# Packed attention products half a step later behind the apart tokens' values, the second scores two half steps later, and the turned blocks' splits ahead of the weights'

## The chip, the cores and the metric

The kernel runs on one core of a Trainium2 chip. The metric is device time in microseconds (us) of one execution; the times before are three runs, 954.72, 954.94 and 955.8 us, with a median of 954.94 us. The engines are TensorE (PE, with its weight loads as PEld), VectorE (DVE), ScalarE (ACT), GpSimd (POOL) and SyncE (SP), which issues most of the DMAs.

## What is computed

Two attention stages in a row (32 packed queries attend to 576 keys, then the 576 queries attend to the 32 packed results), then a two-dimensional Fourier transform over tokens and channels, a normalisation and a two-layer network:

```python
p_packed = sm_attn(p, k, v)                 # 8 batches x 8 heads, 32 packed queries, 576 keys, 64 channels
out = sm_attn(q, p_packed, p_packed)
x = out.transpose(0, 2, 1, 3).reshape(8, 576, 512)
mixed = np.real(np.fft.fft(np.fft.fft(x, axis=1), axis=2))
u = x + mixed
un = (u - mean(u)) / np.sqrt(var(u) + 1e-6)
return u + np.maximum(un @ w_ch1, 0.0) @ w_ch2        # 512 -> 2048 -> 512
```

The kernel keeps about full fp32 accuracy in the network by splitting each operand into a high and a low part and making three matmuls out of one.

## The kernel before

The rows of u are cut into 36 blocks of 128: four for each of the 8 batches (even and odd combinations of tokens), and one for every pair of batches with the 2 x 64 "apart" tokens that fit into no other block. Four blocks make a tile of 512 rows, so there are 9 tiles, 0 to 8. `ffn` runs the network over one tile: for j from 0 to 15, `up(j)` makes 12 matmuls of 128x512 (`ph`, line 958) and `down(j - 1)` 12 more (`acc`, line 977). After each `up` and each `down` stands a call of `step`, so that a tile has 32 half steps, 0 to 31: `step(2j)` lies between `up(j)` and `down(j - 1)`, `step(2j + 1)` between `down(j - 1)` and `up(j + 1)`.

In these half steps the attention and the Fourier transform of the next batch are woven in. `front(b)` is a generator, and each `step` asks it for its next piece; the string `ORDER` says which pieces come, with "y" for the end of a half step. In tile t, `front(t + 1)` runs this way, and two half steps are given to the end of `front(t)` instead: the apart tokens' spectra and their values. The letters of the string for batches from 2 on that matter here:

- V, S, D: load the values, scores of the packed queries, scores out to memory and back turned (`e1T`, two tensors of four DMAs each; the first is issued by SP, the second by ACT in half step 2)
- p0, p1: `packed`, the product of the turned scores with the values (`po`, line 434), normalised by DVE into `pp` (line 439) for each of the two groups of heads
- d0, d1: `packed_parts`, a transpose on PE (`pptp`, line 454), copies and splits of it (`ppT`, `pph`, `ppl`)
- g0, g1: `values_spectrum`, matmuls `pg` (lines 521 and 522), two multiplications on DVE for each (`turned`, line 529) and, one half step later, a split by ACT and POOL (`gh`, `gl`)
- U: `queries`, the second scores (`s2Tt`, `s2T`, line 338) and their transposes on DVE (line 480)
- e, m: the softmax's maximum, exponential and mean

The apart tokens' values are `px<-bd,fa` (line 693), with `xa` and `ubuf` on DVE behind them (lines 714 and 865), and for odd batches a sum for the statistics (line 867). Each `packed`, `pptp`, `pg`, `px` or score takes a PSUM bank out of a ring of three by the name `ps`; `ph` has one bank and `acc` four. The order on PE, DVE, ACT and POOL is the order of the program; SP's is a scheduler's.

At the end of a tile the next tile's blocks are split: `send` (DVE lines 882 and 885, then DMAs `far` and `back`) has turned most of them through memory in half steps 4, 5, 12 and 27, and `parts(i)` makes `uh` on ACT and `ul` on DVE (lines 107 and 110) out of `back`. The weights are split all along, twice for each j: `wr_h` on ACT, `wr_l` on POOL (also lines 107 and 110), with buffers for three pairs.

Of the kernel before, what the change touches and what calls it, by code (L numbers as in the profile page):

```python
# [14 lines left out]
ALU = mybir.AluOpType  # L15
AX = mybir.AxisListType

P = 128
S = 576
HS = S // 2  # L20
D = 64
NPK = 32
# [19 lines left out]
         "i20 d1 w1 m0 q1 e1 T3 a0 f0 i120 g0 j0 r0 w2 w3 c0 w4 w5 i40 g1 m1 P0 w6 X0 j1 a1 f1 c1 r1 P1 X1 v2 W10 P2 w7 T2",  # L42
         "K0 K1 Q0 Q1 y S V0 V1 y X y p0 p1 y d0 d1 y g0 y U y g1 y e0 y e1 y y m0 y a0 y m1 y a1 y f0 y r0 y h0 y f1 y r1 y "
         "h1 y y",
         "V0 V1 S D y X Q0 Q1 y p0 p1 y d0 d1 y g0 y U y g1 y e0 y e1 y y m0 y a0 y m1 y a1 y f0 y r0 y h0 y f1 y r1 y "
         "h1 y y")


# [35 lines left out]
def tile_kernel(ctx, tc, kpT, qT, v, w1, w2, tabS, tabH, tabL, tabR, tabF, tabB, tabT, sel, ident_d, out):  # L84
    nc = tc.nc
# [151 lines left out]
    now = {}  # L237
# [54 lines left out]
    def front(b):  # L292
        kps, vts, qts, e1s, e1T, rinv, away = {}, {}, {}, {}, {}, {}, {}
# [131 lines left out]
        def packed(g):  # L425

            if g not in vts:
                load_values(g)
            vt = vts[g]
            po = bank("po")  # L430
            for c in range(5):
                kk = chunk_rows(c)
                for h in range(4):
                    nc.tensor.matmul(  # L434
                        po[h * NPK:(h + 1) * NPK, :D], e1T[g][:kk, h, c, :],
                        vt[c][:kk, h * D:(h + 1) * D], start=(c == 0), stop=(c == 4),
                        tile_position=(0, h * NPK))
            pp2 = work.tile([P, 2, D], F32, tag="pp2", name="pp2")
            nc.vector.tensor_scalar(pp2, po[:, :D].unsqueeze(1).to_broadcast([P, 2, D]), rinv[g], None, ALU.mult)
            pp2s[g] = pp2  # L440

            def spread():
                mask, n = (bpair, 2) if b else (bmask, 4)
                bd[g] = work.tile([P, n, D], F32, tag=f"bd{n}", name="bd")
                nc.gpsimd.tensor_tensor(bd[g], pp2[:, 0:1, :].to_broadcast([P, n, D]), mask.unsqueeze(2).to_broadcast([P, n, D]),
                                        ALU.mult)

            in_place("b", g, spread)
# [477 lines left out]
    def wsplits():  # L926

        for t, _ in enumerate(tiles):
            for n, j in [(0, 0)] + [x for j in range(1, NJ) for x in ((0, j), (1, j - 1))] + [(1, NJ - 1)]:
# [4 lines left out]
                yield  # L934

    def ffn(first, turned, step, nxt, alone):
        keys = turned.keys
        n = len(keys)
        T = n * P
        uh, ul = turned.hl  # L940
        acc = [psf.tile([P, DM], F32, tag=f"acc{i}", name=f"acc{i}") for i in range(n)]
        now["acc"] = acc

        def up(j, moves=(), between=lambda: None):
            moves = list(moves)
            wh, wl = ready.pop(0)

            pool, tag = (ps, "ps") if alone and j % 2 else (psf, "ph")
            ph = pool.tile([P, 512], F32, tag=tag, name="ph")

            step = T // 2 if first == 0 and j < SPL else T
            for t in (slice(i, i + step) for i in range(0, T, step)):
                for k in range(12):
                    if step < T:
                        c, (l, r) = k % 4, ((wh, uh), (wl, uh), (wh, ul))[k // 4]
                    else:
                        c, (l, r) = k // 3, ((wh, uh), (wh, ul), (wl, uh))[k % 3]
                    nc.tensor.matmul(ph[:, t], l[:, c * P:(c + 1) * P], r[:, c, t], start=(k == 0), stop=(k == 11))  # L958
                    if moves:
                        moves.pop(0)()  # L960
            between()
            hh = ffp.tile([P, 512], F32R, tag="hh", name="hh")
            hl = ffp.tile([P, 512], F32R, tag="hl", name="hl")
            nc.scalar.activation(hh[:, :T], ph[:, :T], AF.Relu)  # L964
            nc.vector.scalar_tensor_tensor(hl[:, :T], ph[:, :T], 0.0, hh[:, :T].bitcast(F32), ALU.max, ALU.subtract)  # L965
            return hh, hl

        def down(j, hh, hl, moves=(), pair=None, to=range(n)):

            moves = list(moves)  # L970
            vh, vl = pair or ready.pop(0)
            for i in to:
                w = slice(i * P, (i + 1) * P)
                halved = nxt is None and j == NJ - 1 and i == n - 1
                for cols in (slice(0, DM // 2), slice(DM // 2, DM)) if halved else (slice(0, DM),):
                    for k, (l, r) in enumerate(((hh, vh), (hh, vl), (hl, vh))):
                        nc.tensor.matmul(acc[i][:, cols], l[:, w], r[:, cols], start=(j == 0 and k == 0),  # L977
                                         stop=(j == NJ - 1 and k == 2 and cols.stop == DM))
                        if moves:
                            moves.pop(0)()  # L980

        def less(*ks):
            for k in ks:
                nxt.less(k)

        def sends(i):
            for _ in range(SENDS.count(i) if nxt is not None else 0):
                nxt.send_next()  # L990

        prev = None
        for j in range(NJ):
            last = nxt is not None and j == NJ - 1
            if last:
                late = [i for i in range(4) if i not in nxt.sent]
                assert len(late) in (0, 1, 2, 4), late
                early = late[:2] if len(late) == 4 else []
                late = [i for i in late if i not in early]
                cur = up(j, [m for i in early for m in nxt.moves(i)], lambda: less(*late))  # L1000
                ahead = [i for i in range(4) if i not in late]
                for i in ahead[:2]:
                    nxt.parts(i)
            else:
                cur = up(j, [lambda: None] * 7 + [turn_others] if first + j == 0 else ())
            next(splits, None)
            if nxt is not None and j == NJ - 2 and not nxt.sent:
                less(0, 1)
            step(2 * j)
            sends(2 * j)  # L1010
            if nxt is None and j == NJ - 1:
                pairs = [ready.pop(0), None]
                down(j - 1, *prev, pair=pairs[0], to=(0, 1))
                pairs[1] = ready.pop(0)
                for k, i in ((1, 0), (1, 1), (0, 2), (1, 2), (0, 3), (1, 3)):
                    down(j - 1 + k, *(prev, cur)[k], pair=pairs[k], to=(i,))
                break
            if prev is not None:
                down(j - 1, *prev, [lambda: None] * 8 + nxt.moves(late[0]) if last and late else ())
                if last:  # L1020
                    for i in ahead[2:]:
                        nxt.parts(i)
                next(splits, None)
                if last:
                    for i in late[:1]:
                        nxt.parts(i)
            step(2 * j + 1)
            sends(2 * j + 1)
            prev = cur
        if nxt is not None:  # L1030
            down(NJ - 1, *prev, nxt.moves(late[1]) if len(late) > 1 else ())
            if len(late) > 1:
                nxt.parts(late[1])
            next(splits, None)
        for i in (2, 3, 0, 1) if nxt is not None else range(4):
            u = u_of[keys[i]]
            for cols in (slice(0, DM // 2), slice(DM // 2, DM)) if nxt is None and i == 3 else (slice(0, DM),):
                nc.vector.scalar_tensor_tensor(u[:, cols], acc[i][:, cols], stat_of[keys[i]][:, 2:3], u[:, cols],  # L1038
                                               ALU.mult, ALU.add)
                (nc.sync if cols.start == 0 else nc.scalar).dma_start(out[(first + i) * P:(first + i + 1) * P, cols], u[:, cols])  # L1040
            free.append(place_of[keys[i]])
# [50 lines left out]
    rest = gen0  # L1092
    for t, (first, tk) in enumerate(tiles):

        gen = gens.pop(t + 1, None) or (front(t + 1) if t + 1 < B else iter(()))
        ended = []

        def step(i):

            next_step()  # L1100
            if i == 2 and t + 1 < B and t:
                now.pop("back")()
            if i in ((1, 2) if t else (0, 2)):
                next(rest, None)
            elif not ended and next(gen, None) == "rest":
                ended.append(gen)
            if t == 0:
                load_weights(i)
            assert i < 2 * NJ - 1 or t + 1 >= B or ended

        nxt = Turned(tiles[t + 1][1]) if t + 1 < len(tiles) else None

        with tc.manual_schedule(engines=MANUAL):
            ffn(first, cur, step, nxt, t + 1 >= B)
        cur, rest = nxt, gen
# [114 lines left out]
```

## Time and profile before

| what | value |
|---|---|
| median of three runs | 954.94 us (954.72 to 955.8) |
| the profiled execution | 953.94 us, of which its span is 952.1 us |
| PE busy | 938.0 us, 99% of the span, 5593 matmuls |
| DVE, ACT, POOL busy | 60%, 47%, 48% |
| DMA, mean | 85 GB/s |
| granted TensorE clock | 0.998 |
| chain that ended last | PE 93%, DMA 2%, DVE 2%, ACT, POOL and issue 1% each |

Matmuls are pipelined, so that a matmul row's duration (some 0.39 us for 128x512) is longer than the distance to the next row's start. The time that a matmul takes from the kernel is read from starts. In the rows of the timeline the first number is the start in us, the second the duration, then engine, line, operation, output and inputs, shapes, a count, and in brackets the idle time just before with what ended it. Tile 0 starts at about 41.7 us, tile 1 at 149.5, tile 2 at 253.8, and the others at 358.2, 461.5, 564.7, 668.0, 771.3 and 860.2 us.

### The profile page before, as it was taken

What the parts mean: (1) busy time and instruction counts of PE and PEld (TensorE: products, weight loads), DVE (VectorE), ACT (ScalarE), POOL (GpSimd) and SP (SyncE); (2) the same over time, 40 slices, a digit from 0 to 9 for tenths busy, and PEclk for the clock granted to TensorE, in tenths of its full rate; (3) what the DMA queues carried; (4) which work ended last, traced back from release to release, by engine and by line L of the source; (5) the groups of instructions that cost most, each with busy time, mean ns of one, the idle gap of its engine ahead of it and who ended that gap; (6) DMA issues with size and microseconds to landing.
All of it is one profiled execution on the core that took longest, in us unless ns stands there. A gap on an engine that the chain in (4) does not pass through costs nothing.

```text
span 952.1 us, 15116 instructions
## 1 busy us (share of the span) xinstructions
PE 938.0 (99%) x5593; PEld 759.1 (80%) x5593; DVE 574.4 (60%) x1171; ACT 444.1 (47%) x909; POOL 453.9 (48%) x392
## 2 busy tenths in 40 slices
PE   7899999999999999999999999999999999999998
PEld 5678887788778887788778877888778878888886
DVE  6789866594758656784678476864678453123112
ACT  4798564444534454444543454454344443233231
POOL 4456444553445444553554354544455355445442
PEclk9999999999999999999999999999999999999999
DMA  9793225200450016200540045100610011001001
GB/s 356 241 349 111 70 88 197 76 1 1 145 175 1 0 53 217 72 1 34 170 138 1 1 144 174 46 1 25 211 41 12 22 46 45 23 23 45 1 0 45
DMA packets 49305, 81.00 MB, mean 85 GB/s; under 512 B 7121, under 2 KB 29137, under 8 KB 49233
## 3 DMA queue, kind: packets, MB, share of 16 engines
q1 hardware_dynamic: 42896, 69.82, 21.8%
q10 hardware_dynamic: 5328, 8.98, 3.0%
q0 software_dynamic: 1008, 1.25, 0.5%
q8 instruction: 44, 0.72, 0.3%
q14 instruction: 29, 0.23, 0.1%
HBM read 59.71 MB, written 20.32 MB: 84 GB/s over the span
## 4 chain that ended last, share of the span: by engine, by line
PE 93%; DVE 2%; DMA 2%; ACT 1%; POOL 1%; issue 1%; ACTq 0%; SPq 0%; DVEq 0%; POOLq 0%
PE acc L977 41%; PE ph L958 40%; PE px L693 2%; PE po L434 1%; DMA w1f<-w 1%; PE py L289 1%; PE py L288 1%; PE py L290 1%; PE py L743 1%; DMA e1T<-fare 1%; PE s2T L338 1%; PE s L338 0%; ACT e L365 0%; PE pz L635 0%; PE pz L658 0%
## 5 line engine op out<-in xcount | busy, mean ns | idle before, releaser
L110 POOL TENSOR_TENSOR wr_l<-w2f,wr_h 128x512 fp32r<-128x512 f32 x144 | 188.4, 1308 | 289.3 <-ACT wr_h L107 267.3
L110 POOL TENSOR_TENSOR wr_l<-w1f,wr_h 128x512 fp32r<-128x512 f32 x144 | 195.3, 1356 | 186.4 <-ACT wr_h L107 160.2
L965 DVE SCALAR_TENSOR_TENSOR hl<-ph,hh 128x512 fp32r<-128x512 f32 x144 | 99.5, 691 | 297.8 <-ACT hh L964 295.4
L977 PE MATMUL acc<-wr_h,hh 128*128 128x512 f32 x577 | 228.5, 396 | 0.0
L958 PE MATMUL ph<-uh,wr_h 128*128 128x512 f32 (+1 forms) x580 | 225.9, 391 | 1.0 <-ACT uh L107 1.0
L977 PE MATMUL acc<-wr_l,hh 128*128 128x512 f32 x577 | 225.3, 390 | 0.0
L977 PE MATMUL acc<-wr_h,hl 128*128 128x512 f32 x577 | 225.1, 390 | 0.0
L958 PE MATMUL ph<-ul,wr_h 128*128 128x512 f32 (+1 forms) x580 | 224.3, 388 | 0.4 <-DVE ul L110 0.4
L958 PE MATMUL ph<-uh,wr_l 128*128 128x512 f32 (+1 forms) x580 | 224.1, 388 | 0.0
L964 ACT ACTIVATE hh<-ph 128x512 fp32r<-128x512 f32 x144 | 86.1, 598 | 243.1 <-PE ph L958 242.8
L107 ACT CAST wr_h<-w1f 128x512 fp32r<-128x512 f32 x144 | 89.3, 620 | 179.8 <-POOL wr_l L110 80.3
L958 PEld LDWEIGHTS ph<-uh,wr_h 128*128 128x128 f32 x580 | 108.5, 188 | 29.1 <-DVE s L480 5.9
L977 PEld LDWEIGHTS acc<-wr_h,hh 128*128 128x128 f32 x577 | 108.3, 188 | 25.3 <-issue 1.6
L977 PEld LDWEIGHTS acc<-wr_h,hl 128*128 128x128 f32 x577 | 108.3, 188 | 23.2
L958 PEld LDWEIGHTS ph<-uh,wr_l 128*128 128x128 f32 x580 | 108.5, 188 | 22.7
L958 PEld LDWEIGHTS ph<-ul,wr_h 128*128 128x128 f32 x580 | 108.6, 188 | 21.7 <-DVE ul L110 0.8
L977 PEld LDWEIGHTS acc<-wr_l,hh 128*128 128x128 f32 x577 | 108.4, 188 | 21.0
L107 ACT CAST wr_h<-w2f 128x512 fp32r<-128x512 f32 x144 | 88.2, 612 | 36.7 <-PE acc L977 23.3
L266 POOL TENSOR_TENSOR stat<-stat,mhalf 128x1 f32<-128x1 f32 x36 | 28.1, 792 | 0.0
L1038 DVE SCALAR_TENSOR_TENSOR ubuf<-acc,stat,ubuf 128x512 f32<-128x512 f32 (+1 forms) x37 | 25.0, 731 | 2.9 <-PE acc L977 2.9
L262 ACT ACTIVATE junk<-ubuf,stat 128x512 f32<-128x512 f32 x36 | 25.8, 717 | 0.1
L110 DVE TENSOR_TENSOR ul<-back,uh 128x512 fp32r<-128x512 f32 x28 | 25.1, 935 | 0.5 <-ACT uh L107 0.2
(222 smaller groups left out, 1081.8 us busy)
## 6 DMA issues: line engine op xcount, KB each, us to landing
kp<-kpT SPq DMA_DIRECT2D x16, 608.0 KB, 5.0
out<-ubuf SPq DMA_DIRECT2D x35, 256.0 KB, 4.0
far<-unt SPq DMA_DIRECT2D x28, 256.0 KB, 2.0
back<-far SPq DMA_DIRECT2D x112, 64.0 KB, 2.0
qt<-qT ACTq DMA_DIRECT2D x12, 576.0 KB, 4.7
vt<-v SPq DMA_DIRECT2D x12, 512.0 KB, 3.9
w1f<-w SPq DMA_DIRECT2D x9, 512.0 KB, 5.6
w2f<-w SPq DMA_DIRECT2D x9, 512.0 KB, 5.8
```

Of the source, the lines that this page charges most:

```text
L107: copied = nc.scalar.copy(hi, src)
L110: (lo_eng or nc.vector).tensor_tensor(lo, src, hi.bitcast(F32), ALU.subtract)
L262: nc.scalar.activation(junk, u, AF.Square, bias=st[:, 1:2], scale=-sign, accum_out=st[:, 2:3])
L266: nc.gpsimd.tensor_tensor(st[:, 2:3], st[:, 2:3], mhalf, ALU.pow)
L288: nc.tensor.matmul(o, lh, rh, start=first, stop=False)
L289: nc.tensor.matmul(o, lh, rl, start=False, stop=False)
L693: nc.tensor.matmul(banks[r][rows, k * 256 + g * P:k * 256 + (g + 1) * P], x[g][at, w], bd[g][at].rearrange("p a d -> p (a d)"), start=True ...
L958: nc.tensor.matmul(ph[:, t], l[:, c * P:(c + 1) * P], r[:, c, t], start=(k == 0), stop=(k == 11))
L964: nc.scalar.activation(hh[:, :T], ph[:, :T], AF.Relu)
L965: nc.vector.scalar_tensor_tensor(hl[:, :T], ph[:, :T], 0.0, hh[:, :T].bitcast(F32), ALU.max, ALU.subtract)
L977: nc.tensor.matmul(acc[i][:, cols], l[:, w], r[:, cols], start=(j == 0 and k == 0), stop=(j == NJ - 1 and k == 2 and cols.stop == DM))
L1038: nc.vector.scalar_tensor_tensor(u[:, cols], acc[i][:, cols], stat_of[keys[i]][:, 2:3], u[:, cols], ALU.mult, ALU.add)
```

## The change

Three edits. First, the string for batches from 2 on gets another "y" ahead of p0, so that p moves from half step 4 to 5, d from 5 to 6, g0 from 6 to 7, and U from 7 to 9; g1 stays in 8, e0 and e1 move by one half step to 10 and 11, and m0 and all behind it stay. Second, for tiles from 1 on the piece of the apart tokens' values moves from half step 2 to 5, where it comes ahead of p, and `packed` writes both groups of heads into two column ranges of one bank, with both normalisations behind the second group. Third, at the end of a tile all blocks that were turned through memory are split at once, ahead of the weights' next split, where two of them came behind it.

```diff
-         "V0 V1 S D y X Q0 Q1 y p0 p1 y d0 d1 y g0 y U y g1 y e0 y e1 y y m0 y a0 y m1 y a1 y f0 y r0 y h0 y f1 y r1 y "
+         "V0 V1 S D y X Q0 Q1 y y p0 p1 y d0 d1 y g0 y g1 y U y e0 y e1 y m0 y a0 y m1 y a1 y f0 y r0 y h0 y f1 y r1 y "
...
-            po = bank("po")
+            if g == 0 or b < 2:
+                po = now["po"] = bank("po")
+            else:
+                po = now["po"]
+            po = po[:, g * D:(g + 1) * D]
...
+            if b < 2:
+                normalized(g, po)
+            elif g == 1:
+                for k in range(2):
+                    normalized(k, now["po"][:, k * D:(k + 1) * D])
+
+        def normalized(g, po):
+
             pp2 = work.tile([P, 2, D], F32, tag="pp2", name="pp2")
-            nc.vector.tensor_scalar(pp2, po[:, :D].unsqueeze(1).to_broadcast([P, 2, D]), rinv[g], None, ALU.mult)
+            nc.vector.tensor_scalar(pp2, po.unsqueeze(1).to_broadcast([P, 2, D]), rinv[g], None, ALU.mult)
...
-                for i in ahead[:2]:
+                for i in ahead:
                     nxt.parts(i)
...
-                if last:
-                    for i in ahead[2:]:
-                        nxt.parts(i)
...
-            if i in ((1, 2) if t else (0, 2)):
+            if i in ((1, 5) if t else (0, 2)):
                 next(rest, None)
-            elif not ended and next(gen, None) == "rest":
+            if i not in ((1, 2) if t else (0, 2)) and not ended and next(gen, None) == "rest":
                 ended.append(gen)
```

On PE, in tile 5, the apart tokens' values stood alone between `up(1)` and `down(0)` before:

```order
L958 MATMUL ph<-uh,wr_h 128x512
L958 MATMUL ph<-ul,wr_h 128x512
L958 MATMUL ph<-uh,wr_l 128x512
L693 MATMUL px<-bd,fa 64x128 x4
L977 MATMUL acc_6271<-wr_h,hh 128x512
L977 MATMUL acc_6271<-wr_l,hh 128x512
```

and the packed products between `up(2)` and `down(1)`; of the change both stand, one behind the other, between `down(1)` and `up(3)` (lines 705, 438, 989 and 970 are the old 693, 434, 977 and 958):

```order
L989 MATMUL acc_6270<-wr_h,hh 128x512
L989 MATMUL acc_6270<-wr_l,hh 128x512
L989 MATMUL acc_6270<-wr_h,hl 128x512
L705 MATMUL px<-bd,fa 64x128 x4
L438 MATMUL po<-vt,e1T 32x64 x16
L438 MATMUL po<-vt_6294,e1T 32x64 x4
L438 MATMUL po<-vt,e1T 32x64 x16
L438 MATMUL po<-vt_6298,e1T 32x64 x4
L970 MATMUL ph<-uh,wr_h 128x512
```

Two places where the network's matmuls are interrupted have become one. On DVE in the same tile the rows from the apart tokens' values to the next `hl` are now these (`xa`, `ubuf` and `stat` belong to the apart tokens, `pp` normalises the packed products, `unp` and `unt` are a send):

```order
L726 TENSOR_TENSOR xa<-px,spec_6360 64x2x128 x2
L877 TENSOR_TENSOR ubuf<-xa,spec_6362 64x256 x2
L879 TENSOR_REDUCE stat<-ubuf 128x1
L257 TENSOR_SCALAR stat<-stat 128x1
L451 TENSOR_SCALAR pp_6518<-po,ri 128x128
L451 TENSOR_SCALAR pp_6522<-po,ri 128x128
L894 TENSOR_SCALAR unp<-ubuf,stat 128x512
L897 STREAM_TRANSPOSE unt<-unp 128x512
L977 SCALAR_TENSOR_TENSOR hl<-ph,hh 128x512
L468 COPY ppT<-pptp 128x128
```

Before, the two normalisations had the `hl` of an `up` ahead of them and the apart tokens' rows stood one `hl` earlier. On ACT at the end of tile 7 the order was

```order
L964 ACTIVATE hh<-ph 128x512
L107 CAST uh<-back 128x4x128 x2
L107 CAST wr_h<-w1f 128x512
L107 CAST uh<-back 128x4x128 x2
L107 CAST wr_h<-w1f 128x512
L107 CAST wr_h<-w2f 128x512
```

and is now

```order
L976 ACTIVATE hh<-ph 128x512
L107 CAST uh<-back 128x4x128 x4
L107 CAST wr_h<-w1f 128x512 x2
L107 CAST wr_h<-w2f 128x512
L976 ACTIVATE hh<-ph 128x512
```

so that the four high parts follow each other and the first weights' split comes two casts later.

More of the change, by code (lines that the diff above doesn't have):

```diff
@@ L434, in packed @@
                     nc.tensor.matmul(
-                        po[h * NPK:(h + 1) * NPK, :D], e1T[g][:kk, h, c, :],
+                        po[h * NPK:(h + 1) * NPK], e1T[g][:kk, h, c, :],
                         vt[c][:kk, h * D:(h + 1) * D], start=(c == 0), stop=(c == 4),
                         tile_position=(0, h * NPK))
+            if b < 2:
[4 more added lines that the diff above has]
+        def normalized(g, po):
             pp2 = work.tile([P, 2, D], F32, tag="pp2", name="pp2")
-            nc.vector.tensor_scalar(pp2, po[:, :D].unsqueeze(1).to_broadcast([P, 2, D]), rinv[g], None, ALU.mult)
+            nc.vector.tensor_scalar(pp2, po.unsqueeze(1).to_broadcast([P, 2, D]), rinv[g], None, ALU.mult)
             pp2s[g] = pp2
```

## The prediction

> **What bounds the kernel now.** First the page's busy times, then the chain of waits, then PE's timeline at the places that the change touches.
>
> ```profile
> span 952.1 us, 15116 instructions
> PE 938.0 (99%) x5593; PEld 759.1 (80%) x5593; DVE 574.4 (60%) x1171; ACT 444.1 (47%) x909; POOL 453.9 (48%) x392
> ```
>
> PE is busy 99% of the span and no other engine over 60%, so the end is set by the sequence of PE's matmuls, and only two things can shorten it: a wait of PE that goes, or a matmul that is spaced more closely to the next. The chain of waits gives the spacing where nothing interrupts:
>
> ```profile
> 456.21 5.44 PE acc L977 x24
> ```
>
> 24 matmuls of 128x512 take 5.44 us, 0.2267 us each. Whatever exceeds this at an interruption is its cost. No matmul is added or removed by the change, so I look for excess.
>
> **Edit 1, the packed products half a step later: a wait goes.** PE's timeline at the packed products of tiles 1, 2 and 4:
>
> ```profile
> 163.49 0.77 PE L434 MATMUL po<-vt,e1T 128*32 128x64 f32 x40
> ...
> 165.28 0.50 PE L977 MATMUL acc<-wr_h,hh 128*128 128x512 f32 x1
> ...
> 267.77 0.77 PE L434 MATMUL po<-vt,e1T 128*32 128x64 f32 x40
> 269.00 0.77 PE L434 MATMUL po<-vt,e1T 128*32 128x64 f32 x40 [0.46 <-DMA e1T<-fare]
> 269.70 0.50 PE L977 MATMUL acc<-wr_h,hh 128*128 128x512 f32 x1
> ...
> 475.42 1.34 PE L434 MATMUL po<-vt,e1T 128*32 128x64 f32 x80
> 476.69 0.50 PE L977 MATMUL acc<-wr_h,hh 128*128 128x512 f32 x1
> ```
>
> In tile 4 the 80 matmuls take 476.69 - 475.42 = 1.27 us; in tile 2 they take 1.93, because the second group's turned scores land late, and in tile 1 they take 1.79. The excess is 0.66 and 0.52, together 1.18 us. (The bracket shows only 0.46, since a row's modelled end hides part of the gap.) Tiles 3 to 6 have no such wait. With the products behind `down(1)` PE comes some 2.72 us (12 matmuls) and the apart tokens' 0.58 (below) later, less the interruption of half step 2 that has gone. That is over 2 us more for a DMA that is 0.7 us late at most. Its issue does not move: it stands in half step 2 on ACT, behind work of half steps 0 and 1. **Term: -1.18 us.** From both sides: 0 if something moved the DMA as well, -1.18 if the wait goes whole; I take -1.18, since 2 us of cover is three times the wait.
>
> **Edit 2, the apart tokens' values in front: one interruption less.** The same view in tile 4, at the values of half step 2:
>
> ```profile
> 468.85 0.39 PE L958 MATMUL ph<-uh,wr_l 128*128 128x512 f32 x1
> 469.17 0.65 PE L693 MATMUL px<-bd,fa 64*64 64x128 f32 x8
> 469.75 0.50 PE L977 MATMUL acc<-wr_h,hh 128*128 128x512 f32 x1
> ...
> 472.60 0.39 PE L958 MATMUL ph<-uh,wr_h 128*128 128x512 f32 x1
> ```
>
> From the last `ph` to the next `up` pass 472.60 - 468.85 = 3.75 us. They hold 13 full matmuls (13 x 0.2267 = 2.95) and the values' own 469.75 - 469.17 = 0.58. The rest, 0.22 us, is paid for going from full matmuls to tiles of the array and back: 469.17 - 468.85 = 0.32 instead of 0.23 going in, and 0.13 spread over the first full matmuls afterwards. The packed products pay the same when alone. If the two stand together, one pair of these is saved, provided that the seam between a 64*64 and a 128*32 tiling costs nothing. The trace has no such seam, but a like one, 64*32 scores followed by 128*32 strips, beside each of them alone:
>
> ```profile
> 464.43 1.06 PE L338 MATMUL s<-kp 64*32 64x512 f32 x16
> 465.43 0.64 PE L658 MATMUL pz<-ysum,tbf 128*32 128x258 f32 x8
> 466.00 0.51 PE L650 MATMUL pz<-yr,tbr 101*128 101x258 f32 x2
> ...
> 486.00 1.06 PE L338 MATMUL s2T<-qt,ppT 64*32 64x512 f32 x16
> 487.00 0.50 PE L958 MATMUL ph<-uh,wr_h 128*128 128x512 f32 x1
> ...
> 774.09 0.64 PE L658 MATMUL pz<-ysum,tbf 128*32 128x258 f32 x8
> 774.67 0.51 PE L650 MATMUL pz<-yr,tbr 101*128 101x258 f32 x2
> ```
>
> Scores take 1.00 us to the next start whether strips follow (465.43 - 464.43) or a full matmul (487.00 - 486.00); the strips take 0.57 behind scores and 0.58 behind a full matmul (tile 7, where no scores precede). So the seam is free, and a group that joins another adds only its body. Both pieces exist in tiles 1 to 6 (tile 7 has no next batch). **Term: 6 x 0.22 = -1.3 us.** From both sides: 0 if the seam costs as much as what it replaces, -1.3 if it is free; I take the like seam's answer.
>
> The Trainium skill, page "TensorEngine Tiling (Array Packing)", section "Key Properties", says that changing the tiling mode drains TensorE, which speaks against a free seam: three changes of mode would stand where four stood, so that half of the 0.22 were saved, 0.7 us in all. In the trace a tiled group's time to the next start is the same before either kind of successor, so that a drain, if there is one, is already in the group's own body.
>
> **What these moves put on other engines.** Everything that moves is issued one or two half steps later with the same successors, so I check who is late next, in tile 5, where an odd batch has the most on DVE:
>
> ```profile
> 574.29 0.77 DVE L714 TENSOR_TENSOR xa<-px,spec 64x256 f32<-64x256 f32 x2
> 575.09 0.95 DVE L865 TENSOR_TENSOR ubuf<-xa,spec 64x256 f32<-64x256 f32 x2
> 576.08 0.69 DVE L867 TENSOR_REDUCE stat<-ubuf 128x1 f32<-128x512 f32 x1
> ...
> 580.08 0.60 DVE L439 TENSOR_SCALAR pp<-po,ri 128x128 f32<-128x128 f32 x2
> 580.60 0.95 DVE L882 TENSOR_SCALAR unp<-ubuf,stat 128x512 f32<-128x512 f32 x1
> 581.59 0.71 DVE L885 STREAM_TRANSPOSE unt<-unp 128x512 f32<-128x512 f32 x1
> ```
>
> All of it now stands between one `hl` and the next. Counted from the end of `px` on PE: 0.77 + 0.95 + 0.69 + 0.60, with some 0.2 for the small operations, gives 3.2 us until `pp` is there. PE asks for it (the transposes of half step 6) after the products and an `up`, 1.27 + 2.72 = 4.0 us at the least. Cover: 0.8 us in odd tiles, 1.5 in even ones without the sum. The send (0.95 + 0.71) ends at about 4.9 us and the `hl` behind it has until the `up` after the next `down`, almost 3 us more. The second scores need banks that `turned` of g1 releases; before, they needed those of g0, at the same distance of half a step. The program lets no wait on POOL or ACT stand before those products.
>
> Of the DMAs, the queries' load is on ACT at the same place, and the sends' `back` goes into buffers that the packed products release, now half a step later. On SP the next batch's keys wait for the second scores, two half steps later; they take 5.0 us and are read a tile later:
>
> ```profile
> kp<-kpT SPq DMA_DIRECT2D x16, 608.0 KB, 5.0
> ```
>
> Behind them stand only sends of half step 12 and later. **Term: 0.**
>
> **Edit 3, the high parts together: the wait at tile 8.** Its first `up`, with the splits ahead of it:
>
> ```profile
> 860.16 0.39 PE L958 MATMUL ph<-uh,wr_h 128*128 128x512 f32 x1
> 860.93 0.50 PE L958 MATMUL ph<-ul,wr_h 128*128 128x512 f32 x1 [0.38 <-DVE ul L110]
> ...
> 866.29 0.39 PE L977 MATMUL acc<-wr_h,hh 128*128 128x512 f32 x1
> ...
> 855.42 1.13 ACT L107 CAST uh<-back 128x512 fp32r<-128x512 f32 x2
> 856.45 0.62 ACT L107 CAST wr_h<-w1f 128x512 fp32r<-128x512 f32 x1
> 856.97 1.14 ACT L107 CAST uh<-back 128x512 fp32r<-128x512 f32 x2
> ...
> 856.16 1.28 DVE L110 TENSOR_TENSOR ul<-back,uh 128x512 fp32r<-128x512 f32 x2
> 857.62 3.25 DVE L110 TENSOR_TENSOR ul<-back,uh 128x512 fp32r<-128x512 f32 x2 [0.18 <-ACT uh L107]
> ...
> 857.15 3.17 POOL L110 TENSOR_TENSOR wr_l<-w1f,wr_h 128x512 fp32r<-128x512 f32 x2 [3.12 <-ACT wr_h L107]
> ```
>
> 24 matmuls take 866.29 - 860.16 = 6.13 us instead of 5.44: 0.69 of excess, for `ul`. The second pair of `ul` takes 3.25 us where the first took 1.28, while POOL makes two `wr_l` over the same stretch. With four casts in a row (0.52 each) the last `uh` is there at about 857.5, and the four `ul` would end near 858.8; POOL's first `wr_l` cannot start before the first `wr_h`, about 858.1, so that only the last `ul` meets it. Even if that one were held until POOL's 1.3 us are over, it ends before 860.2, and PE asks at 860.39. The weights' low part of j = 0 ends at about 859.6, and PE's third matmul asks for it at 860.6. **Term: -0.69 us**; from both sides 0 and -0.69. The other tiles' ends show no excess, and their splits become earlier.
>
> **Sum.** -1.18 - 1.3 - 0.69 = -3.2 us. Against the profiled execution (953.94 us with 1.8 us around its span) that is 950.8. That execution lies 1.0 us below the median of the runs, 954.94; against the median I forecast 951.7 us.
>
> **Rivals.**
>
> 1. The seam is not free. By half the saving edit 2 gives 0.7 and the time is 952.4; if it pays the whole 0.22, 953.1. For it: no 64*64 group is followed by a 128*32 one in the trace. Against: both sides of the like seam. Chance 0.16, of which 0.04 for the whole.
> 2. One of the two waits stays (the DMA's at 1.18, or `ul` at 0.69): 952.4 to 952.9. For it: SP's order is a scheduler's, and DVE and POOL still meet at the last `ul`. Chance 0.07.
> 3. Slower: the second scores wait for the buffers of `turned`. g0 and g1 now follow each other at once, and the three `tmp` buffers hold g0's first product until POOL has made `gl` from it. If g1's second product had to take that buffer, it would wait for POOL:
>
> ```profile
> 593.37 0.60 ACT L964 ACTIVATE hh<-ph 128x512 fp32r<-128x512 f32 x1 [3.16 <-PE ph L958]
> 593.86 0.61 ACT L107 CAST wr_h<-w2f 128x512 fp32r<-128x512 f32 x1
> 594.55 1.31 POOL L110 TENSOR_TENSOR wr_l<-w2f,wr_h 128x512 fp32r<-128x512 f32 x1 [2.23 <-ACT wr_h L107]
> ```
>
> `hh` starts at 593.37, so that the `up` ahead of g1 is over by then. POOL is through with the weights at 595.85 and with `gl` (516 columns to the weights' 512, so 1.3 again, an estimate) at 597.2; the product (like an `ul`, 0.64) would be there at 597.8, 4.5 us after. PE wants its bank after g1's four matmuls of 258 columns (half a full one each, 0.46) and a `down` (2.72), some 3.2 us after. Six waits of 1.3 us, +7.8, on the forecast give 959.5. It decides as soon as that wait is over 0.5 us per tile. Against it: g0's second product leaves its buffer free when the two are joined, and the program's wait before g1's second product names DVE and PE alone. Chance 0.05.
> 4. DVE's cover of 0.8 us fails in the odd tiles, because the operations stretch beside POOL as `ul` did: 0.3 to 1 us in each of three tiles, 952.6 to 954.7. Chance 0.04.
>
> **How the numbers follow.** The forecast has 0.68. Its own range is 951.2 to 952.2; rivals 1 and 2 reach 953.1, which closes the range above; below, the runs differ by up to 1 us, and I go to 950.9. A measurement tells about 0.2%, 1.9 us, from no change, so faster means under 953.0: the forecast, 0.12 of rival 1, rival 2 and half of rival 4, 0.89, from which I take 0.02 for what I have not thought of. Same: 0.08. Slower: 0.05.
>
> **What would show it.** In PE's timeline of the changed kernel: no bracket with `e1T` at the packed products, and 1.27 us for them in tiles 1 and 2; `px` and `po` adjacent, with 0.58 us from the first `px` to the first `po`, and one excess of 0.22 where there were two; 5.44 us for the first 24 matmuls of tile 8. Wrong would be: more than 0.6 us from `px` to `po` (rival 1), idle time before `pptp` (rival 4), or before `s2T` (rival 3). The prediction as a whole is wrong if PE's span shrinks by less than 1.9 us.

## The result, and the profile after

The changed kernel takes 960.44 us (median of 6 runs, 960.19 to 962.0) where the kernel before took 954.83 us beside it (6 runs, 954.36 to 955.8). The ratio is 1.0061, 95% interval 1.0048 to 1.0074: slower by 0.6%, where 951.7 us and "faster" had been forecast. The profiled execution took 960.28 us. The ratios are of executions at a granted clock of 0.995 or more; one execution each of experiments 1 and 3, at 0.557 and 0.85 (1563 and 1040 us), stands in the medians alone. In what follows, line numbers of the changed kernel are 12 higher than those of before from behind the packed products' matmuls on (`up` is L970, `down` L989, the joins of `turned` L547; the matmuls themselves are L438).

The head of its page:

```profile
span 958.3 us, 15122 instructions
...
PE 936.3 (98%) x5593; PEld 760.1 (79%) x5593; DVE 577.7 (60%) x1171; ACT 444.2 (46%) x909; POOL 450.6 (47%) x392
```

The span is 6.2 us longer, with the same 5593 matmuls and the same granted clock, 0.998. So PE waits more. The view of waits (engine, line, what it waited for: us in total, times, longest) names the new one in its first row:

```profile
PE ph L970 <- DVE s L492: 9.1, 6, 1.5
```

Six times, once in each of tiles 1 to 6, `up(5)` waits up to 1.5 us for DVE's transposes of the second scores. No wait of PE for anything like it stood in the kernel before. PE's timeline in tile 5, first at the place of the first two edits, then at the new wait:

```profile
585.07 0.65 PE L705 MATMUL px<-bd,fa 64*64 64x128 f32 x8
585.65 1.34 PE L438 MATMUL po<-vt,e1T 128*32 128x64 f32 x80
586.92 0.50 PE L970 MATMUL ph<-uh,wr_h 128*128 128x512 f32 x1
...
599.35 0.34 PE L338 MATMUL s2Tt<-qt,ppT 64*32 64x64 f32 x16
599.48 1.06 PE L338 MATMUL s2T<-qt,ppT 64*32 64x512 f32 x16
602.06 0.47 PE L970 MATMUL ph<-uh,wr_h 128*128 128x512 f32 x1 [1.51 <-DVE s L492]
```

The first three rows are as forecast: values and products adjacent, 0.58 us from the first `px` to the first `po`, 1.27 from there to the `up`, no bracket. The last three are the loss: from the first `s2T` to the `up` pass 602.06 - 599.48 = 2.58 us, where 1.00 passed before (2.57 to 2.59 in the six tiles, where 0.99 to 1.00 passed). Six times 1.58 is 9.5 us. The `ph` bank itself is what is missing: `s2Tt`, the tail of the second scores, was written into it for one of the two groups of heads, and the bank is free only when DVE has transposed that tail.

The chain of waits says what DVE was doing instead (start, us, what):

```profile
597.52 1.30 DVE turned L541 x2
598.82 0.02 issue
598.84 0.04 DVE turned L547
598.88 1.36 issue
600.24 1.52 DVE turned L547
601.75 0.17 DVE s L492
601.92 0.14 issue
602.06 2.97 PE ph L970 x12
```

Two joins of 128x258, the sum and the difference of the second group's products, stand between the products and the transposes. Beside the timelines of DVE and of POOL over the same microseconds (DVE's three rows, then POOL's):

```profile
597.52 1.29 DVE L541 TENSOR_TENSOR turned<-pg,turn 128x516 f32<-128x516 f32 x2
598.84 2.92 DVE L547 TENSOR_TENSOR turned<-turned 128x258 f32<-128x258 f32 x2
601.68 0.37 DVE L492 STREAM_TRANSPOSE s<-s2Tt 128x64 f32<-128x64 f32 x2
...
597.46 1.31 POOL L110 TENSOR_TENSOR wr_l<-w2f,wr_h 128x512 fp32r<-128x512 f32 x1 [1.96 <-ACT wr_h L107]
598.73 1.30 POOL L110 TENSOR_TENSOR gl<-turned,gh 128x516 fp32r<-128x516 f32 x1
599.99 1.48 POOL L110 TENSOR_TENSOR wr_l<-w1f,wr_h 128x512 fp32r<-128x512 f32 x1
```

The same place before, where the scores stood behind the *first* group's join:

```profile
588.61 0.77 DVE L535 TENSOR_TENSOR turned<-turned 128x258 f32<-128x258 f32 x2
589.57 0.38 DVE L480 STREAM_TRANSPOSE s<-s2Tt 128x64 f32<-128x64 f32 x2 [0.19 <-PE s2Tt L338]
...
589.76 1.30 POOL L110 TENSOR_TENSOR wr_l<-w1f,wr_h 128x512 fp32r<-128x512 f32 x1 [1.22 <-ACT wr_h L107]
591.01 1.31 POOL L110 TENSOR_TENSOR gl<-turned,gh 128x516 fp32r<-128x516 f32 x1
```

Two joins take 0.77 us before and 2.92 after; before, they are over while POOL stands still, and DVE then waits for the scores. After, `gl` runs to 598.73 + 1.30 = 600.03 and the first join ends at 600.24 to 600.31; `wr_l` runs to 601.47 and the second ends at 601.76. Each join is done some 0.3 us behind the end of a POOL instruction, of the 0.42 us that a join takes alone, so that it did most of its work when POOL's was over. The reason that `gl` is there at all: the split of a group follows one half step behind its product, and g1 now follows g0 by one half step, where it followed by two.

The first row holds the counter-example: the products, which take one input from PSUM (`pg`), run beside POOL's `wr_l` all the way, and take 0.69 us each (1.29 for the two, which overlap). The first product of g0 in tile 5 has POOL beside it for 0.41 us only and takes 0.70, so that the time doesn't grow with POOL's share. An operation with a single large input in SBUF can be held all the same. A send's `unp` takes 0.48 us at 796.54, where POOL is idle, and this beside a `wr_l` that started 0.06 us before it and ended at 585.19:

```profile
583.94 1.52 DVE L894 TENSOR_SCALAR unp<-ubuf,stat 128x512 f32<-128x512 f32 x1
```

**Theory A**: DVE's joins, with both inputs in SBUF, are shut out while POOL runs, and the second scores' transposes queue behind them. **Theory B**: rival 3 of the prediction, the second group waits for a buffer that POOL's `gl` has to release. **Theory C**: the second scores are simply too late in their new half step, whatever POOL does. The Trainium skill, page "SBUF — State Buffer", section "Who interferes with whom", states what A needs: a DVE instruction with two SBUF inputs contends with a GpSimd instruction that reads SBUF, because its second input comes through a read interface that the two share, and one with at most one SBUF input does not, outside the modes in which it uses both ports. The rows above agree, with 0.42 to 1.5 us for the joins and 0.69 to 0.70 us for the products; `unp` shows that the condition on the modes, or something like it, matters here, but no run tells in which mode it ran.

### The profile page after: what moved, and what is told of

Same layout as the page of the kernel before. It is cut to its first block, busy times and chain, and to the rows that moved or that the text cites. A ratio compares the mean times of both kernels' runs of the same rounds, so it can differ in the third digit from the quotient of the medians.

```text
span 958.3 us, 15122 instructions
## 1 busy us (share of the span) xinstructions
PE 936.3 (98%) x5593; PEld 760.1 (79%) x5593; DVE 577.7 (60%) x1171; ACT 444.2 (46%) x909; POOL 450.6 (47%) x392
## 4 chain that ended last, share of the span: by engine, by line
PE 92%; DVE 3%; issue 2%; ACT 1%; DMA 1%; POOL 1%; SPq 0%; DVEq 0%; ACTq 0%; POOLq 0%
PE ph L970 41%; PE acc L989 40%; PE px L705 2%; DVE turned L547 1%; PE po L438 1%; DMA w1f<-w 1%; DVE turned L541 1%; PE py L289 1%; PE py L288 1%; PE py L290 1%; PE py L755 1%; PE s L338 1%; PE pz L670 0%; PE pz L647 0%; ACT hh L976 0%
## 5 line engine op out<-in xcount | busy, mean ns | idle before, releaser
L110 POOL TENSOR_TENSOR wr_l<-w1f,wr_h 128x512 fp32r<-128x512 f32 x144 | 197.8, 1374 | 177.0 <-ACT wr_h L107 140.3
L970 PE MATMUL ph<-uh,wr_h 128*128 128x512 f32 (+1 forms) x580 | 226.5, 392 | 10.1 <-DVE s L492 9.1
L989 PE MATMUL acc<-wr_h,hh 128*128 128x512 f32 x577 | 227.7, 395 | 0.0
L989 PE MATMUL acc<-wr_l,hh 128*128 128x512 f32 x577 | 225.4, 391 | 0.0
L989 PE MATMUL acc<-wr_h,hl 128*128 128x512 f32 x577 | 225.3, 391 | 0.0
L970 PE MATMUL ph<-ul,wr_h 128*128 128x512 f32 (+1 forms) x580 | 224.6, 389 | 0.0
L970 PE MATMUL ph<-uh,wr_l 128*128 128x512 f32 (+1 forms) x580 | 224.5, 389 | 0.0
L970 PEld LDWEIGHTS ph<-uh,wr_h 128*128 128x128 f32 x580 | 108.6, 188 | 38.9 <-issue 14.4
L989 PEld LDWEIGHTS acc<-wr_h,hh 128*128 128x128 f32 x577 | 108.4, 188 | 23.8 <-issue 0.4
L970 PEld LDWEIGHTS ph<-uh,wr_l 128*128 128x128 f32 x580 | 108.6, 188 | 22.7
L989 PEld LDWEIGHTS acc<-wr_h,hl 128*128 128x128 f32 x577 | 108.4, 188 | 22.7
L989 PEld LDWEIGHTS acc<-wr_l,hh 128*128 128x128 f32 x577 | 108.5, 188 | 21.4
L970 PEld LDWEIGHTS ph<-ul,wr_h 128*128 128x128 f32 x580 | 108.7, 188 | 20.6
L266 POOL TENSOR_TENSOR stat<-stat,mhalf 128x1 f32<-128x1 f32 x36 | 25.5, 720 | 0.0
L547 DVE TENSOR_TENSOR turned<-turned 128x258 f32<-128x258 f32 x28 | 24.4, 910 | 0.5
```

Of the source, the lines that this page charges most:

```text
L110: (lo_eng or nc.vector).tensor_tensor(lo, src, hi.bitcast(F32), ALU.subtract)
L266: nc.gpsimd.tensor_tensor(st[:, 2:3], st[:, 2:3], mhalf, ALU.pow)
L547: TW[TA[min(b, 2)]].tensor_tensor((prod[0] if b else hi)[:, t, :], prod[0][:, t, :], prod[1][:, t, :], ops[t])
```

## The experiments

**1. The first group's split one half step later.** From the changed kernel:

```diff
-                    after(1, lambda: split(hi, lo, prod[0], TW[TL[min(b, 2)]]))
+                    after(2 if b > 1 and g == 0 else 1, lambda: split(hi, lo, prod[0], TW[TL[min(b, 2)]]))
```

> Edit to the changed kernel: the split of the first group's transposed block (gh on ACT, gl on POOL) is issued one half step later in tiles 2 to 6 (tile 1 has it at the old place); everything else stays. Theory A (DVE's join of the second group meets POOL's gl of the first and is held by it): without gl beside them the joins of the second group fall from 1.47 and 1.52 us towards the 0.42 of before, wholly if gl alone does it, and at least the first of the two if the weights' wr_l still meets the second; the 16 products s2T of the second scores go back from 2.58 to 1.0 us; time 960.4 - 5 x 1.58 = 952.5 us if both joins are free, about 956 if only one is. Theory B (rival 3 of the prediction: the second group's products wait until POOL has released the buffers with gl): gl comes 2.7 us later, so the wait grows to over 2.6 us in tiles 2 to 6, 960.4 + 5 x 2.7 = 974 us, and in any case not below 960. Theory C (the second scores simply come too late for DVE, whatever POOL does): 960.4, unchanged.

It was 952.0 us, ratio to the kernel before 0.9972 (0.9960 to 0.9984). The expectation counts tiles 2 to 6, but `b > 1` takes in tile 1 as well (in the profile below its joins take 0.43 and 0.42 us), so that six waits go and its sum should have been 960.4 - 6 x 1.58 = 950.9. The same kernel once more:

> The kernel with the first group's split one half step later once more, for a profile at the full clock (the first one had 0.557). Theory A: joins at 0.42 to 0.43, s2T at 1.0 us in tiles 1 to 6, no wait of PE for DVE's transposes; time 0.996 to 0.998 of before, about 952.3 us. Theory B: s2T at 2.6 us or more at the full clock, where PE asks earlier than it did at 0.557, and 960 us or more.

Again 0.9972 (0.9963 to 0.9982), 952.07 us. DVE's, POOL's and PE's timelines in tile 5:

```profile
594.31 0.77 DVE L547 TENSOR_TENSOR turned<-turned 128x258 f32<-128x258 f32 x2
595.27 0.38 DVE L492 STREAM_TRANSPOSE s<-s2Tt 128x64 f32<-128x64 f32 x2 [0.19 <-PE s2Tt L338]
...
592.93 1.31 POOL L110 TENSOR_TENSOR wr_l<-w2f,wr_h 128x512 fp32r<-128x512 f32 x1 [1.96 <-ACT wr_h L107]
595.45 1.31 POOL L110 TENSOR_TENSOR wr_l<-w1f,wr_h 128x512 fp32r<-128x512 f32 x1 [1.21 <-ACT wr_h L107]
596.70 2.59 POOL L110 TENSOR_TENSOR gl<-turned,gh 128x516 fp32r<-128x516 f32 x2
...
594.95 1.06 PE L338 MATMUL s2T<-qt,ppT 64*32 64x512 f32 x16
595.95 0.50 PE L970 MATMUL ph<-uh,wr_h 128*128 128x512 f32 x1
```

The joins are back at 0.77 for both, in the gap that POOL has between 594.24 and 595.45, and the scores take 595.95 - 594.95 = 1.00 us. Both joins are free with `gl` alone gone, since the first no longer holds the second back into `wr_l`. The edit moves ACT's `gh` along with `gl`, but in the changed kernel `gh` was over at 597.91, before the first join began at 598.84, so that it isn't what held the joins. The groups of the second scores (count, min/median/max in ns, first to last start in us), for the kernel before, the changed one and this one, show it over five tiles:

```profile
L338 PE MATMUL s2T<-qt,ppT x96: 588/589/589, 174.6 to 693.0; 64*32 64x512 f32 x96
```

```profile
L338 PE MATMUL s2T<-qt,ppT x96: 588/589/590, 180.1 to 704.6; 64*32 64x512 f32 x96
```

```profile
L338 PE MATMUL s2T<-qt,ppT x96: 589/589/589, 181.8 to 698.5; 64*32 64x512 f32 x96
```

From tile 1's second scores to tile 6's pass 518.4 us before, 524.5 after and 516.7 here. The prediction's terms for these five tiles, 5 x 0.22 and tile 2's 0.66, come to -1.8, and 518.4 - 1.8 = 516.6. With five waits of 1.58 it is 524.5. Theory A holds; B, which had the wait grow, falls, and so does C, which had 960.4.

**2. A fourth buffer for the products.** One number, in all places that share the tag:

```diff
-                tag, n = ("ln", 2) if b == 0 and g == 1 else ("tmp", 3)
+                tag, n = ("ln", 2) if b == 0 and g == 1 else ("tmp", 4)
```

> Edit to the changed kernel: four buffers instead of three for the 128x516 products (tag tmp) and what shares them; nothing else. Theory A (a port or lock that DVE and POOL share): unchanged, joins 1.5 us, s2T 2.58 us, 960.4 us. Theory B (rival 3: the second group has to wait until a buffer is released by POOL's gl): the wait goes, s2T 1.0 us, 951 us.

961.82 us (two runs), ratio 1.0078 (1.0060 to 1.0096), and PE's wait is the same:

```profile
PE ph L970 <- DVE s L492: 8.9, 6, 1.5
```

No buffer is missing. B falls a second time.

**3. `gl` in two halves, at the same place.** The work on POOL is the same, cut into two instructions:

```diff
-                    after(1, lambda: split(hi, lo, prod[0], TW[TL[min(b, 2)]]))
+                    after(1, halves)
+
+            def halves():
+                nc.scalar.copy(hi, prod[0])
+                for t in range(2):
+                    TW[TL[min(b, 2)]].tensor_tensor(lo[:, t, :], prod[0][:, t, :], hi[:, t, :].bitcast(F32), ALU.subtract)
```

> Edit to the changed kernel: gl is made by two instructions of 128x258 on POOL in place of one of 128x516, at the same place. Theory A1 (DVE's join is shut out for the whole of a POOL instruction and gets in between two): the first join gets in behind the first half, the second behind the second half, so that both are done some 1.1 us earlier (600.6 instead of 601.75 in tile 5); s2T falls from 2.58 to about 1.5 us, the time by 6 x 1.1 to about 954 us. Theory A2 (both engines share a bandwidth and both slow down in proportion): the joins stay at about 1.5 us, s2T at 2.5, the time at 960. Theory B: gl ends a little later with two starts, 960 to 961.

954.38 us, ratio 0.9999 (0.9990 to 1.0008). DVE, POOL and PE in tile 5 (lines behind the edit are another 5 higher):

```profile
594.62 1.81 DVE L547 TENSOR_TENSOR turned<-turned 128x258 f32<-128x258 f32 x2
...
594.51 1.64 POOL L554 TENSOR_TENSOR gl<-turned,gh 128x258 fp32r<-128x258 f32 x2
596.12 1.49 POOL L110 TENSOR_TENSOR wr_l<-w1f,wr_h 128x512 fp32r<-128x512 f32 x1
...
595.27 1.06 PE L338 MATMUL s2T<-qt,ppT 64*32 64x512 f32 x16
596.75 0.47 PE L975 MATMUL ph<-uh,wr_h 128*128 128x512 f32 x1 [0.41 <-DVE s L492]
```

The joins take 1.81 us for both, not 2.92, and the scores 596.75 - 595.27 = 1.48, not 2.58: 1.1 us less, as A1 had said, and 6 x 1.1 = 6.6 of the 9.5 us. The length of the POOL instruction that a join meets sets its delay. Each engine gets in between the other's instructions, and POOL pays too: the two halves of `gl` take 1.64 us here and 1.44 where no join meets them (at 597.56), `wr_l` 1.49 for 1.31. A bandwidth shared in proportion (A2) would have left the joins as they were.

**4. The second scores ahead of both groups.**

```diff
-         "V0 V1 S D y X Q0 Q1 y y p0 p1 y d0 d1 y g0 y g1 y U y e0 y e1 y m0 y a0 y m1 y a1 y f0 y r0 y h0 y f1 y r1 y "
+         "V0 V1 S D y X Q0 Q1 y y p0 p1 y d0 d1 y U y g0 y g1 y e0 y e1 y m0 y a0 y m1 y a1 y f0 y r0 y h0 y f1 y r1 y "
```

> Edit to the changed kernel: the second scores go back from half step 9 to half step 7, ahead of both groups, which take half steps 8 and 9. Theory A (what is late is the transposes of the second scores, queued on DVE behind the second group's joins): the joins stay long, 1 us or more each, but the scores no longer stand behind them, so that s2T falls to 1.0 us and the time to 960.4 - 6 x 1.58 = 951.0 us, 950.9 to 952.5; a wait of PE behind the second group may come up elsewhere, at most what the joins' 2.1 us exceed the next 2.7 us of up by, so none. Theory B (a buffer of the second group): the wait moves to the second group's own next user, PE's interpolation in half step 12, and the scores are free: also near 951, so this run doesn't tell A from B. Theory C (the scores of an odd half step always wait there, because DVE is late in the whole stretch): s2T stays at 2.5 us and the time at 960.

952.65 us, ratio 0.9983 (0.9975 to 0.9992). The joins of the second group still meet `gl`, and nobody waits for them:

```profile
597.48 2.00 DVE L547 TENSOR_TENSOR turned<-turned 128x258 f32<-128x258 f32 x2
...
597.70 1.50 POOL L110 TENSOR_TENSOR gl<-turned,gh 128x516 fp32r<-128x516 f32 x1
```

The second of the pair takes 1.53 us. The scores take 1.02 to 1.19 us in the six tiles, and PE has no wait in this stretch of tile 5. The time is a little above the expected 950.9 to 952.5. What the scores take beyond 1.00 us comes to 0.6 us over the six tiles; why they take longer is open. So the contention costs time only through what stands behind it on DVE. That the scores are now in an odd half step of their own, 7, does not separate their place from POOL's work; experiments 1 and 3, which leave them in half step 9, do, and C falls by those.

**5. The joins on POOL.**

```diff
-TA = (0, 1, 1)
+TA = (0, 1, 0)
```

> Edit to the changed kernel: the joins of the blocks from tile 1 on are made by POOL itself, not by DVE, so that no DVE join can meet POOL's work. Theory A: DVE's queue ahead of the second scores' transposes loses 2 x 1.5 us, s2T goes to 1.0 us, and the time to about 951 to 953 us if POOL, busy 48%, has room for four more operations of some 1.3 us per tile, with gl of the second group that much later. Theory B (buffers released by POOL): POOL releases them later still, the wait grows, over 965 us. Theory C: unchanged, 960.

952.32 us, ratio 0.9977 (0.9968 to 0.9986). The group's row (min/median/max in ns):

```profile
L547 POOL TENSOR_TENSOR turned<-turned x24: 736/743/761, 177.7 to 699.3; 128x258 f32<-128x258 f32 x24
```

On POOL a join takes 0.74 us, undisturbed 1.75 times DVE's 0.42, but half of what DVE took when it met POOL. The scores are at 0.99 to 1.00 us in all six tiles.

**6. Without the delay of the packed products; and the high parts alone.** The first goes back to the half steps of before for all pieces (`p0 p1` in half step 4 with the values), and keeps the other two edits:

```diff
-         "V0 V1 S D y X Q0 Q1 y y p0 p1 y d0 d1 y g0 y g1 y U y e0 y e1 y m0 y a0 y m1 y a1 y f0 y r0 y h0 y f1 y r1 y "
+         "V0 V1 S D y X Q0 Q1 y p0 p1 y d0 d1 y g0 y U y g1 y e0 y e1 y y m0 y a0 y m1 y a1 y f0 y r0 y h0 y f1 y r1 y "
...
-            if i in ((1, 5) if t else (0, 2)):
+            if i in ((1, 4) if t else (0, 2)):
```

> Edit to the changed kernel: the packed products go back to the end of half step 4, with groups and second scores in the half steps of before (6, 8, and scores in 7 between them); the values in front of the products and the high parts ahead of the weights stay. Theory A: no second scores stand behind a join that meets POOL, s2T is at 1.0 us in all tiles; the seam saves 6 x 0.22 = 1.3 and tile 8 saves 0.69, while the wait for e1T stays (0.52 + 0.66, perhaps some 0.3 us more each, as PE is earlier): 955 - 2 = 953.0 us, 952.6 to 953.6. Theory B: the same. Theory C (the merged values and products load DVE so that the scores are late whatever the order): s2T over 1.5 us here too, and over 956 us.

953.35 us, ratio 0.9990 (0.9979 to 1.0002), and the scores take 1.00 us in all six tiles; C had over 956. The second is the kernel before with the third edit only:

```diff
-                for i in ahead[:2]:
+                for i in ahead:
                     nxt.parts(i)
...
-                if last:
-                    for i in ahead[2:]:
-                        nxt.parts(i)
```

> The kernel before with the third part of the change alone: the turned blocks' high parts ahead of the weights' at a tile's last steps; half steps, products and values as before. By the prediction's term: the first 24 up matmuls of tile 8 take 5.44 us instead of 6.13, and the time falls by 0.69, to 954.1 of 954.8, within 0.2% of before. If the four casts in a row delay the first wr_h, PE's wait for wr_l takes the place of that for ul there, and the time is 954.8 or more.

954.21 us, ratio 0.9996 (0.9987 to 1.0005), too small to tell from nothing by its time. PE's timeline tells it: tile 8's first `up`, and the `down` that follows 24 matmuls later.

```profile
861.07 0.39 PE L958 MATMUL ph<-uh,wr_h 128*128 128x512 f32 x1
...
866.51 0.39 PE L977 MATMUL acc<-wr_h,hh 128*128 128x512 f32 x1
```

5.44 us, as forecast. These two kernels, both without the delay, also show that the wait for `e1T` moves about. In the profile before it stood in tiles 1 and 2. PE's timeline without the delay, in tile 3, and then that of the high parts alone, in tile 2:

```profile
370.41 0.65 PE L705 MATMUL px<-bd,fa 64*64 64x128 f32 x8
371.16 0.77 PE L438 MATMUL po<-vt,e1T 128*32 128x64 f32 x40
372.18 0.77 PE L438 MATMUL po<-vt,e1T 128*32 128x64 f32 x40 [0.24 <-DMA e1T<-fare]
372.88 0.50 PE L989 MATMUL acc<-wr_h,hh 128*128 128x512 f32 x1
```

```profile
268.78 0.77 PE L434 MATMUL po<-vt,e1T 128*32 128x64 f32 x40
269.72 0.77 PE L434 MATMUL po<-vt,e1T 128*32 128x64 f32 x40 [0.17 <-issue]
270.42 0.50 PE L977 MATMUL acc<-wr_h,hh 128*128 128x512 f32 x1
```

The first needs 372.88 - 370.41 = 2.47 us for values and products that take 0.58 + 1.27 = 1.85 elsewhere, and the second 270.42 - 268.78 = 1.64 for products that take 1.27. Over all tiles the excess is 1.1 us in the one (0.62 in tile 3, 0.49 in tile 5) and 0.61 in the other (0.37, 0.15 and 0.09 in tiles 2, 3 and 5), beside 1.18 in the profile before. The view names the DMA for one of these waits only, and ACT or issue for two others. That they are for `e1T` is read from the landings: in tiles 3 and 5 of the one and 2 and 5 of the other the last of its transfers lands 0.05 to 0.25 us ahead of the second group of products, where 0.34 to 0.61 us lie between in tiles 3 to 6 of the profile before, which have no excess. For the 0.15 us in tile 3 of the other it isn't shown.

## Why the prediction was wrong

Three of its terms came true in the profile, and the one that it set to nothing outweighed them.

- **Edit 1, the wait for `e1T`, -1.18**: gone. The packed products take 1.27 us in tiles 1 to 6. The size was that of one execution: those of the two other kernels without the delay show 1.1 and 0.61.
- **Edit 2, one interruption less, -1.3**: right, and so is the seam. 0.58 us from `px` to `po`, then 1.27. Beyond these, 0.23 us for `px` and 0.24 to 0.25 for `po` in tiles 3 to 6 have become 0.23 to 0.27 for both. Rival 1 is out. The like seam of the prediction could not have shown this by itself, because both successors of its scores change the tiling. The drain at a change of mode, by which the Trainium skill's page "TensorEngine Tiling (Array Packing)", section "Key Properties", spoke against the saving, costs no time of its own at this seam.
- **Edit 3, the wait at tile 8, -0.69**: gone, 5.43 us in the changed kernel and 5.44 in experiment 6.
- **"What these moves put on other engines ... Term: 0"** is the step that failed. Its sentence on the second scores was "The second scores need banks that `turned` of g1 releases; before, they needed those of g0, at the same distance of half a step." It followed banks that the scores' matmuls *write*, and those were free: PE did the scores on time. It didn't follow who reads them: the transposes stand on DVE behind g1's joins, and `up(5)` needs the `ph` bank that holds the scores' tail. And "the same distance" compared half steps, not what POOL does in them: behind g0 POOL's gap, behind g1 the `gl` of g0. The joins, at 0.42 us each, were not in the sum at all. What that step should have read is +6 x 1.58 = +9.5 us.
- **The sum**: -3.2 + 9.5 = +6.3 us; the spans differ by 958.3 - 952.1 = 6.2.
- **Rival 3** had the place (second scores behind g1, POOL's `gl` beside it), six waits, and nearly the time (959.5 us), but the wrong mechanism, a buffer; a fourth buffer changed nothing. It was dismissed on the grounds that hold against a buffer only. **Rival 4** had the mechanism (DVE's operations stretch beside POOL, as `ul` did) but looked for it ahead of the transposes of half step 6, where PE shows no wait. The cover there was thinner than the prediction's 0.8 us: in tile 5 `pp` is done at 589.36 and PE asks at 589.79, because the `unp` of 1.52 us shown above stands ahead of these operations. The row that should have joined the two rivals was in the prediction itself: the pair of `ul`, 3.25 us beside two `wr_l` where 1.28 was its own time.

With the contention taken away and all three edits kept, experiment 1 is the forecast's case: 0.9972 of 954.94 us is 952.3 us, 0.6 from the forecast and inside its range. That version is faster than both kernels: than the changed one by about 8 us, than the kernel before by some 2.7 (0.16% to 0.40%).

## What to carry to other kernels

When work moves to another half step, list for every engine not only who produces and frees what it needs, but which instructions will stand ahead of the consumer in its queue, and what POOL runs during them: here a short DVE operation with two SBUF inputs that came behind the start of a POOL instruction lasted until some 0.3 us after that one's end, and so did `unp`, which has one. A forecast of nothing for side effects deserves the same row-by-row sum as the gains, above all when every gain is under 1.5 us. If such a meeting can't be avoided, move the POOL work by a half step, cut it into shorter instructions, or see that nothing urgent stands behind it on DVE; here the first took all six waits away (9.5 us by the rows, about 8 by the medians) and the second 6.6 us of them (about 6 by the medians).

## What the runs showed of the hardware

- A join of 0.42 us took 1.47 to 1.53 us beside POOL instructions of 1.3 us, and 0.91 to 0.97 beside halves of them: DVE's row in the profile contains the time for which it is shut out. The two engines take turns when both have work queued: POOL's `wr_l` took 1.48 instead of 1.30 us in the same meeting. The Trainium skill's section cited above calls this an exclusive lock, and the halves agree with that: shorter instructions, shorter waits. Which one is held goes by who started first: at tile 8 of the changed kernel the last `ul` (128x512, two SBUF inputs) started 0.22 us ahead of a `wr_l` and took 0.69 us as when alone, and the `wr_l` took 1.63.
- A product of DVE with one input in PSUM was not slowed beside the same POOL instructions: 0.68 to 0.70 us each, with POOL at work for 0.41 us of it or for all. A tensor_scalar with its one large input in SBUF (`unp`) took 1.52 instead of 0.48.
- A 64*64 tiling followed by a 128*32 one cost nothing extra at the seam: 0.58 us for `px` whether products or full matmuls followed, and one excess of 0.23 to 0.27 us where two had stood.
- PE's wait for the `e1T` transfers differs between the profiles of the three kernels without the delay: none, 0.37 and 0.66 us in tile 2.
